# Fixed sort keys for the first part, latest-start keys behind it

## The chip, the cores and the metric

The kernel runs on one core of one Trainium2 chip. The metric is the device time of one execution in microseconds; a version is timed in several executions, and the median is given.

## What is computed

Three layers, each feeding the next, all in float32 on the inputs and outputs:

```python
# 1. retention: 4 batches, 8 heads, 576 positions, 64 dims
scores = scale * (q @ k.T)
ret = (scores * gamma ** rel where rel >= 0 else 0) @ v
x = ret, heads side by side              # 2304 x 512
# 2. first feed-forward layer, 512 -> 2048 -> 512
h = x @ w_in;  x = (h * cos(h)) @ w_out
# 3. second feed-forward layer, 512 -> 2048 -> 512
h = x @ w_in2; out = softplus(h) @ w_out2
```

## The kernel before

Matmuls work on pairs of a high and a low part of each operand (three products for one), so every activation and weight is split before use: ScalarE makes the high part, VectorE or GpSimd subtracts it to make the low one.

**The stages.** Retention is cut into 32 pieces (`piece`): scores (L625), running states (L630, L634), masks on VectorE (L652, L666), states on VectorE (L684), values (L702), then the split of the result into x (ScalarE L737, VectorE L349). The first 16 pieces run alone; the other 16 are spread over the first three of five token groups of layer 1's first part. That part, `moe_a`, multiplies each group by 4 of the 16 blocks of layer 1's weights: L789 into hidden units, then the chain ScalarE L824, VectorE L828, ScalarE L831, VectorE L834, ScalarE L859, VectorE L349 (`gl`), and L880 out of it. Its weights are made in SBUF by `weight` (ScalarE L423 and L429, VectorE L435, ScalarE L488 `wh`, VectorE or GpSimd L349 `wl`). The other blocks are converted ahead (`convert_ahead`: L423, L438, L442) and stored to DRAM. From then on the work is done in quads (L987, seven products in place of eight) with L1399 (layer 1) or L1150 (layer 2) multiplying out of them. The fifth group of the first part runs between the first quads.

**The order.** Nothing is ordered by hand. Every operation is entered into a `Plan` with an engine, a duration, a sort key and its tiles. `schedule` simulates the engines: at each step it takes the operation that can start earliest on its engine, and among those that could start at the same time the one with the smallest key. A piece of retention is one operation of TensorE there, so its readers count as ready when the whole piece is done. `latest` then walks backward from the planned TensorE times, works out how late each operation may begin, and writes that over the sort key of every ScalarE, VectorE and GpSimd operation; this is done twice before the last run of `schedule`. In that last run a second rule, with the constant `LOOK`, lets an operation go ahead of the chosen one if it would otherwise be late and the chosen one has room. The resulting order is emitted as the instruction streams; on the chip each engine works through its stream in that order and waits on semaphores. The chip does not know the planned times.

The fixed keys that matter here come from these lines, where `M[m]` is the nominal start of token group m (M[0] = M0 = 28.07) and a group's four slots are spaced by `slot_a(m)`, 7.02 for the first group:

```python
piece([i], [i], range(done, i), M[m] - 6.0 + y * FA * slot_a(m) / count)
        masks(i, K + 0.8)      # states: K + 0.4, after (x): K + 1.8
weight(1, f, W0[0] + W0[1] * f, W0[2])          # L435 at k + 0.6, wl at k + 2.8
        k = M[0] + CA[0] + 4 * i * CA[2]        # convert_ahead; L438 at k + 0.6
            op("dve", t_dve(n), K1 + 0.6, a2, ...)   # L828; K1 = slot start + 2.77
```

Of the kernel before, what the change touches and what calls it, by code (L numbers as in the profile page):

```python
# [66 lines left out]
    return layer == 2 or f < FA  # L67


FLEX = 1.332  # L70
FLEX_AD = 3.889
FLEX_2 = 50.0
ROOM = 258.786
SPARE = 1.248
# [6 lines left out]
GB = 2  # L81
PT = 3
R0 = 26.837
WB = (16.258, 19.07)
W3 = (33.511, 10.601, 13.324, 18.951, 18.328)
XW = 15.747
XC = 10.657
LAG_C = 1.399
LAG_S = 0.9
TT = 3  # L90
CA = (26.164, 78.45, 5.342, 6.693)
TURN = 0.6
XS = 51.414
FILL = (2, 5)
EARLY = 14.073
EARLY_2 = 4.87
PASSES = 2
LOOK = 0.5
LO_A = "pool or dve"
END = 3.1  # L100
LC = 8.411
LT = ("o", "s")
OFF = (-1.482, 8.354, 20.766, 32.756)
LL = 12.0
LB = 1.9
WARM = 350
DX = 24.051
LEAD = 7.302
W0 = (46.735, 4.619, -0.157)
M0 = 28.072  # L110
AK = (4.689, 2.82)
PAIR_A = 1.48
ALONE = 4
LENT = (0, 2)
# [3 lines left out]
KK = 1.331  # L118
KQ = -0.176
TIE = -8.153  # L120
LAG = -2.74
LEAD_G = 8.451
CX = 0.855
GT = (4, 7)
LS = 9
LEAD_S = 11.446
W4 = (-20.151, -4.061, 13.456, -5.221, 0.968)
W5 = (15.439, 11.845, 7.768, 11.854, 3.532)
PAD = 192
QS = 3  # L130

# [1 line left out]
class Plan:  # L133
# [65 lines left out]
    def latest(self, order, after):  # L199

        late, total = [0.0] * len(self.ops), max(self.end)
        for i in reversed(order):
            e, nbytes = self.eng[i], self.ops[i][6]
            if e == "pe":
                late[i] = self.start[i]
                continue
            lf = min((late[j] - (0.14 if self.eng[j] == e else self.LAT[e]) for j in after[i]), default=total)
            late[i] = lf - (1.7 + nbytes / 365e3 + LATE if nbytes else self.end[i] - self.start[i])
        for i, o in enumerate(self.ops):
            if self.eng[i] in ("act", "dve", "pool"):  # L210
                o[2] = late[i]
        return late

    def schedule(self, behind, loose, after, next_, late):
        n = len(self.ops)
        left = [0] * n
        for i, o in enumerate(self.ops):
            left[i] = len(o[4]) + len(behind[i])
        ready = [0.0] * n
        free, port, link = dict.fromkeys(("pe", "act", "dve", "pool", "sp", "host"), 0.0), 0.0, 0.0  # L220
        can = [i for i in range(n) if not left[i]]
        start, end, self.eng = [0.0] * n, [0.0] * n, [None] * n
        window, busy, warm = 0, 0.0, False
        for _ in range(n):
            best = None
            for i in can:
                eng, dur, key, _, _, uses_port, _ = self.ops[i]
                if eng == POOL_DVE:
                    f = max(ready[i], port)
                    t, d, e = min(  # L230
                        ((max(f, free[e]), d, e) for e, d in (("pool", t_pool(dur)), ("dve", t_dve(dur)))),
                        key=lambda o: o[0] + (FLEX if ready[i] < ROOM else FLEX_2 if ready[i] < ROOM_3 else FLEX_3) * o[1])
                elif eng == ACT_DVE:
                    t, d, e = min(
                        ((max(ready[i], free[e], port if e == "dve" and uses_port else 0.0), d, e) for e, d in zip(("act", "dve"), dur)),
                        key=lambda o: o[0] + FLEX_AD * o[1] + (SPARE if o[2] == "dve" else 0.0))
                else:
                    t, d, e = max(free[eng], ready[i], port if uses_port else 0.0, key - LEAD if eng == "sp" else 0.0), dur, eng
                k = (t, key, i, d, e)
                if best is None or k < best:  # L240
                    best = k
            assert best is not None, "the plan has a cycle"
            t, _, i, dur, eng = best
            if late and LOOK and eng in ("act", "dve"):
                more = None
                for j in can:
                    e, d, key = self.ops[j][:3]
                    if j != i and e == eng and ready[j] < t + dur:
                        f = max(free[eng], ready[j], port if self.ops[j][5] else 0.0)
                        if f < t + dur and late[j] < t + dur + LOOK and f + d + LOOK < late[i] and (more is None or (late[j], f, j) < more[0]):  # L250
                            more = (late[j], f, j), d
                if more:
                    (_, t, i), dur = more
            can.remove(i)
            what, _, _, _, _, uses_port, nbytes = self.ops[i]
            start[i], self.eng[i] = t, eng
            at, left_ = t, dur if eng == "pe" else 0.0
            while left_ > 1e-9:
                edge = (window + 1) * CLOCK_WINDOW
                if at >= edge:  # L260
                    warm = busy > (0.42 if warm else 0.75) * CLOCK_WINDOW
                    window, busy = window + 1, 0.0
                    continue
                run = min(edge - at, left_ * (1 if warm else 2))
                at, busy, left_ = at + run, busy + run, left_ - run / (1 if warm else 2)
            if eng == "pe":
                dur = at - t
            free[eng] = end[i] = t + dur
            if uses_port and eng != "act" or what == POOL_DVE:
                port = t + dur  # L270
            if nbytes:
                link = max(link, t + 1.7) + nbytes / 365e3
                end[i] = link + (0.95 if t < 60.0 else LATE)
            for j in next_[i]:
                ready[j] = max(ready[j], t)
                left[j] -= 1
                if not left[j]:
                    can.append(j)
            for j in after[i]:
                same = self.ops[j][0] == eng and not nbytes  # L280
                ready[j] = max(ready[j], end[i] + ((0.0 if (j, i) in loose else self.OWN.get(eng, 0.0)) if same else self.LAT[eng]))
                left[j] -= 1
                if not left[j]:
                    can.append(j)
        self.start, self.end = start, end
        return sorted(range(n), key=lambda i: (start[i], i))
# [11 lines left out]
def retention_moe_moe(ctx, tc, qkv, w1, w2, mask, mtail, dq, dk, out):  # L298
# [205 lines left out]
    def weight_out(q, key):  # L504
# [10 lines left out]
        for j in range(2):  # L515
            k = key + j * W3[4]
            ok, ov = oks[j], ovs[j]
# [442 lines left out]
    def quad(ph, y, s):  # L960
# [43 lines left out]
        product(1, 1, K, True, True)  # L1004
        op(ACT_DVE, both, K + DT - EARLY, keep(1, 0, "v"), r=[rk[1], ("qopen",)], w=[(cv, 0)], new=[("cv", 1, cv)])
        product(2, 2, K + DT, True, True)
        product(3, 5, K + 2 * DT, True, True)
        op("dve", t_dve(HN), K + 3 * DT - EARLY_2, lambda: nc.vector.tensor_tensor(R(2), R(2), c["v"][:, 0], ALU.add), r=[(cv, 0)], w=[rk[2]])
        op(ACT_DVE, both, K + 3 * DT - EARLY, keep(3, 0, "5"), r=[rk[3], ("qopen",)], w=[(cv, 0)])
        product(1, 6, K + 3 * DT)  # L1010
        op(ACT_DVE, both, K + 4 * DT - EARLY, keep(1, 1, "v"), r=[rk[1]], w=[(cv, 1)])
        product(3, 3, K + 4 * DT)
# [5 lines left out]

        op("dve", t_dve(HN), K + 6 * DT - EARLY, fourth, r=[rk[1], (cv, 0)], w=[rk[4]], new=free(4))
        op("dve", t_dve(HN), K + 5 * DT - EARLY_2, lambda: nc.vector.tensor_tensor(R(3), R(3), c["v"][:, 1], ALU.add), r=[(cv, 1)], w=[rk[3]])  # L1020
        product(1, 4, K + 6 * DT)
# [281 lines left out]
    def weight_in_s(ph, y, s):  # L1303
# [6 lines left out]
        wk = wof(ph, y, q)  # L1310
        W = (W3, W4, W5)[ph]
        slot_ = c % 2
        zd = NP2 * (layer - 1) + q
        made = (wk, "made")
        key = KI(ph, y, s) - (W[0] if y == 0 and s < 2 else W[1] if y == 0 or ph else XW)

# [304 lines left out]
    for i in range(P0):  # L1621
        k = M[0] + CA[0] + 4 * i * CA[2]
        job(k, convert_ahead, 1, FQ[0] + i, k, CA[2])
    for q in range(NP2):
        k = CM[0] + CA[1] + 4 * q * CA[3]
        job(k, convert_ahead, 2, q, k, CA[3])
    for ph in range(3):
        W = (W3, W4, W5)[ph]
        for y in range(nb):
            k = KI(ph, y, 0) - XC  # L1630
            job(k, x_load, ph, y, k)
            for s in range(NQ[ph]):
                job(KI(ph, y, s), quad, ph, y, s)
                job(KI(ph, y, s) - max(0.1, W[0] if y == 0 and s < 2 else W[1] if y == 0 or ph else XW), weight_in_s, ph, y, s)
                if not ph:
# [5 lines left out]
        for q in range(NQ[ph]):  # L1641
            if ph:
                job(key_s(ph, 0, 0, q) - max(W[4 if q > 1 else 2], 0.1), weight_out_s, ph, q)
            else:
                k = unit_key(0, 0, q) - W3[2]
                job(max(k, (MR if q < 2 else MB) + 0.01), weight_out, FQ[0] + q, k)
# [83 lines left out]
```

## Time and profile before

| what | value |
|---|---|
| median of 3 runs | 834.55 us (831.53 to 835.55) |
| the profiled execution's own time | 835.85 us |
| its span, first to last instruction | 834.1 us |
| TensorE busy | 818.9 us, 98% |
| VectorE / ScalarE / GpSimd busy | 665.3 / 513.3 / 76.6 us |
| mean granted clock of TensorE | 0.996 |

The profiled execution's own time is 1.75 us longer than the span. TensorE's busy time counts overlapping matmuls once, and a matmul at half clock is busy for twice as long, so the busy share says little on its own; the idle time and the granted clock by stretch say where time is lost.

### The profile page before, as it was taken

What the parts mean: (1) busy time and instruction counts of PE and PEld (TensorE: products, weight loads), DVE (VectorE), ACT (ScalarE), POOL (GpSimd) and SP (SyncE); (2) the same over time, 40 slices, a digit from 0 to 9 for tenths busy, and PEclk for the clock granted to TensorE, in tenths of its full rate; (3) what the DMA queues carried; (4) which work ended last, traced back from release to release, by engine and by line L of the source; (5) the groups of instructions that cost most, each with busy time, mean ns of one, the idle gap of its engine ahead of it and who ended that gap; (6) DMA issues with size and microseconds to landing.
All of it is one profiled execution on the core that took longest, in us unless ns stands there. A gap on an engine that the chain in (4) does not pass through costs nothing.

```text
span 834.1 us, 15908 instructions
## 1 busy us (share of the span) xinstructions
PE 818.9 (98%) x5792; PEld 781.5 (94%) x5792; DVE 665.3 (80%) x1486; ACT 513.3 (62%) x1128; POOL 76.6 (9%) x99
## 2 busy tenths in 40 slices
PE   8999999899999999999999999999999999999998
PEld 5777788888999999999999999999999999999998
DVE  3788667988989756876577889879788999876896
ACT  1275554567877866767767776555565766554551
POOL 3631010200402010010101010000000000000000
PEclk9999999999999999999999999999999999999999
DMA  9797999898788989486958967715558585563313
GB/s 302 297 353 242 333 395 325 295 397 323 286 306 257 340 305 328 156 231 230 299 200 261 312 213 224 264 66 204 214 175 329 210 303 199 175 233 127 139 51 114
DMA packets 74797, 208.78 MB, mean 250 GB/s; under 512 B 6880, under 2 KB 31072, under 8 KB 70880
## 3 DMA queue, kind: packets, MB, share of 16 engines
q1 hardware_dynamic: 71264, 203.06, 67.1%
q0 software_dynamic: 3456, 4.72, 3.8%
q8 instruction: 45, 0.74, 0.4%
q14 instruction: 32, 0.26, 0.1%
HBM read 129.64 MB, written 78.12 MB: 249 GB/s over the span
## 4 chain that ended last, share of the span: by engine, by line
PE 70%; DVE 1%; ACT 0%; DMA 0%; issue 0%; DVEq 0%
PE acc L1150 22%; PE ha L987 19%; PE acc L1399 16%; PE s L987 9%; PE hb L987 5%; DMA wr<-in_w 0%; DVE tt L1552 0%; DVE pair L349 0%; DVE er L828 0%; ACT pair L1270 0%; DVE s L1020 0%; DVE o L1017 0%; DVE gs L834 0%; ACT gh L859 0%; ACT wr L429 0%
## 5 line engine op out<-in xcount | busy, mean ns | idle before, releaser
L987 PE MATMUL ha<-x,pair 128*128 128x384 f32 x1008 | 202.8, 335 | 0.5 <-DVE o L1017 0.5
L987 PEld LDWEIGHTS ha<-x,pair 128*128 128x128 f32 x1008 | 174.5, 188 | 2.3 <-DVE o L1017 0.8
L1399 PE MATMUL acc<-gh,pair 128*128 128x384 f32 x576 | 155.4, 334 | 0.0
L1150 PE MATMUL acc<-pair,gh 128*128 128x256 f32 x544 | 106.7, 283 | 0.0
L1399 PEld LDWEIGHTS acc<-gh,pair 128*128 128x128 f32 x576 | 104.8, 188 | 0.0
L987 PE MATMUL s<-x,pair 128*128 128x384 f32 x504 | 101.2, 335 | 0.5 <-DVE gl L349 0.4
L1399 PE MATMUL acc<-gl,pair 128*128 128x384 f32 x288 | 96.4, 335 | 0.4 <-DVE gl L349 0.4
L987 PEld LDWEIGHTS s<-x,pair 128*128 128x128 f32 x504 | 88.0, 188 | 1.3 <-DVE gl L349 0.7
L1150 PEld LDWEIGHTS acc<-pair,gh 128*128 128x128 f32 x544 | 84.6, 191 | 0.0
L1150 PE MATMUL acc<-pair,ah 128*128 128x256 f32 x408 | 81.7, 281 | 0.0
L1150 PE MATMUL acc<-pair,gl 128*128 128x256 f32 x272 | 76.8, 282 | 0.0
L831 ACT ACTIVATE er<-er,hp_t 128x384 f32<-128x384 f32 (+1 forms) x92 | 57.4, 628 | 15.1 <-DVE er L828 14.7
L1150 PEld LDWEIGHTS acc<-pair,ah 128*128 128x128 f32 x408 | 66.5, 190 | 0.2 <-DVE pt L1197 0.2
L1150 PE MATMUL acc<-pair,al 128*128 128x256 f32 x204 | 57.7, 283 | 0.0
L353 ACT ACTIVATE cv<-ha 128x384 f32<-128x384 f32 x84 | 41.0, 488 | 26.4 <-PE ha L987 26.1
L349 DVE TENSOR_TENSOR gl<-sf,gh 128x512 fp32r<-128x512 f32 x68 | 46.9, 689 | 10.6 <-ACT gh L1128 9.9
L1399 PEld LDWEIGHTS acc<-gl,pair 128*128 128x128 f32 x288 | 54.1, 188 | 0.8 <-DVE gl L349 0.7
L1128 ACT ACTIVATE gh<-sf 128x512 fp32r<-128x512 f32 x68 | 43.0, 632 | 18.3 <-DVE sf L1093 12.4
L1150 PEld LDWEIGHTS acc<-pair,gl 128*128 128x128 f32 x272 | 52.0, 191 | 0.0
L987 PE MATMUL hb<-x,pair 128*128 128x384 f32 x252 | 50.6, 335 | 0.0
L423 ACT ACTIVATE wy<-wr 128x512 f32<-128x512 f32 x64 | 42.5, 665 | 8.8 <-DVE wk L435 3.1
L987 PEld LDWEIGHTS hb<-x,pair 128*128 128x128 f32 x252 | 43.6, 188 | 0.0
(209 smaller groups left out, 1684.1 us busy)
## 6 DMA issues: line engine op xcount, KB each, us to landing
wr<-in_w SPq DMA_DIRECT2D x64, 512.0 KB, 6.5
pair<-wpd SPq DMA_DIRECT2D x16, 1792.0 KB, 7.0
wpd<-pair SPq DMA_DIRECT2D x14, 1792.0 KB, 8.0
wd<-wk SPq DMA_DIRECT2D x56, 256.0 KB, 5.1
pair<-wd SPq DMA_DIRECT2D x36, 256.0 KB, 5.6
sd<-x SPq DMA_DIRECT2D x12, 768.0 KB, 4.3
x<-sd SPq DMA_DIRECT2D x12, 768.0 KB, 7.2
raw<-in_qkv SPq DMA_DIRECT2D x12, 640.0 KB, 6.9
```

What stands on the lines that cost most here:

```text
L349: e.tensor_tensor(out_, a, hi.bitcast(F32), ALU.subtract)
L353: nc.scalar.activation(out_, in_, AF.Copy)
L423: nc.scalar.activation(y, T["wr", u][:, :, 1].bitcast(F32), AF.Prelu, scale=2.0 ** -112, alpha=2.0 ** 32)
L831: nc.scalar.activation(e["r"], e["r"], AF.Sin, bias=hp_t[:, 0:1], scale=TWO_PI)
L987: nc.tensor.matmul(R(r), w_(a), x_(b), start=(start and n == 0), stop=(n == 5), skip_group_check=True)
L1128: nc.scalar.activation(T[hk], T[fk], AF.Copy)
L1150: nc.tensor.matmul(acc[m][:, i * 256:i * 256 + 256], l[p], r[o], start=(s == 0 and i == 0 and n == 0), stop=(s == half_p - 1 and n == 2), ...
L1399: nc.tensor.matmul(acc[m][:, 0:HN], l[:, z_], e[r], start=(first and z == 0), stop=(last and z == 2))
```

## The change

A constant `LATE_FROM = 150.0` is added, a time in the plan's own microseconds. Operations of ScalarE, VectorE and GpSimd that the plan starts before it keep the fixed key that they were entered with; only those after it get the latest-start key. The second rule (`LOOK`) works only behind that time too. That point lies at the end of the spread pieces of layer 1's first part, about where the first quad begins. Beside it 14 constants or tuples that make up keys and thresholds get new values. No operation is added or removed, and no tile, buffer count or transfer size is changed.

```diff
-FLEX = 1.332
-FLEX_AD = 3.889
+FLEX = 1.319
+FLEX_AD = 3.856
-WB = (16.258, 19.07)
-W3 = (33.511, 10.601, 13.324, 18.951, 18.328)
-XW = 15.747
-XC = 10.657
+WB = (16.86, 21.855)
+W3 = (33.09, 10.062, 18.026, 16.22, 18.284)
+XW = 18.07
+XC = 10.621
-CA = (26.164, 78.45, 5.342, 6.693)
+CA = (23.719, 75.53, 5.342, 4.427)
-EARLY = 14.073
-EARLY_2 = 4.87
+EARLY = 13.944
+EARLY_2 = 8.541
-LOOK = 0.5
+LOOK = 0.32
+LATE_FROM = 150.0
-OFF = (-1.482, 8.354, 20.766, 32.756)
-LL = 12.0
+OFF = (-1.221, 10.539, 20.766, 32.756)
+LL = 10.179
-W0 = (46.735, 4.619, -0.157)
+W0 = (46.735, 4.227, -0.157)
-AK = (4.689, 2.82)
+AK = (4.689, 2.701)
-LAG = -2.74
-LEAD_G = 8.451
+LAG = -3.013
+LEAD_G = 7.778
-LEAD_S = 11.446
-W4 = (-20.151, -4.061, 13.456, -5.221, 0.968)
-W5 = (15.439, 11.845, 7.768, 11.854, 3.532)
+LEAD_S = 10.241
+W4 = (-19.467, -8.868, 14.452, -5.177, 15.14)
+W5 = (16.461, 18.885, 9.073, 12.575, 2.839)
...
         for i, o in enumerate(self.ops):
-            if self.eng[i] in ("act", "dve", "pool"):
+            if self.eng[i] in ("act", "dve", "pool") and self.start[i] > LATE_FROM:
                 o[2] = late[i]
...
-            if late and LOOK and eng in ("act", "dve"):
+            if late and LOOK and eng in ("act", "dve") and t > LATE_FROM:
                 more = None
```

## Rows read from the trace of the kernel before

**Rows 1.** Busy time by engine in stretches, with granted clock (PEclk) and DMA share:

```profile
core 0: us, PE busy (x) PEld busy (x) DVE busy (x) ACT busy (x) POOL busy (x), PEclk, DMA share, GB/s
...
40.00:80.00 40.00, 36.47 (x361) 28.55 (x359) 35.06 (x82) 27.42 (x61) 8.90 (x12) 0.97 0.78 278
80.00:120.00 40.00, 40.00 (x297) 32.19 (x294) 26.32 (x64) 20.20 (x43) 3.55 (x6) 0.99 0.99 367
...
160.00:260.00 100.00, 96.12 (x513) 89.50 (x512) 90.31 (x158) 75.35 (x148) 16.23 (x13) 1.00 0.90 338
260.00:830.00 570.00, 570.00 (x3755) 569.27 (x3755) 458.31 (x1025) 361.14 (x801) 21.32 (x24) 1.00 0.64 218
```

**Rows 2.** Waits of TensorE: line waited for, us in total, times, longest:

```profile
PE s L625 <- DVE st L684: 3.5, 2, 2.0
PE o L789 <- DVE gl L349: 2.2, 1, 2.2
...
PE ha L987 <- DVE o L1017: 0.5, 1, 0.5
PE s L987 <- DVE gl L349: 0.4, 1, 0.4
PE acc L1399 <- DVE gl L349: 0.4, 1, 0.4
PE acc L880 <- ACT pt L353: 0.4, 1, 0.4
```

**Rows 3.** Busy time by engine behind the second stall, columns as in the first group:

```profile
76.00:81.00 5.00, 4.29 (x46) 3.46 (x47) 4.19 (x13) 1.84 (x3) 0.24 (x1) 0.66 0.98 298
```

**Rows 4.** Timeline of VectorE from 72.5 us: start, us, instruction, idle before it:

```profile
72.53 1.39 DVE L442 SCALAR_TENSOR_TENSOR wk<-wr,wk 128x512 int32<-128x512 int32 x1
73.85 0.68 DVE L828 CUSTOM_DVE_ANT_0 er<-ek,hb 128x512 f32<-128x512 int32 x1
74.45 0.41 DVE L652 TENSOR_TENSOR p<-s,m_t 128x256 f32<-128x256 f32 x1
74.78 0.27 DVE L684 SCALAR_TENSOR_TENSOR st<-st,dk_t,s 128x64 f32<-128x64 f32 x1
75.58 0.42 DVE L652 TENSOR_TENSOR p<-o,m_t 128x256 f32<-128x256 f32 x1 [0.54 <-ACT x L737]
...
76.39 0.27 DVE L684 SCALAR_TENSOR_TENSOR st<-st,dk_t,s 128x64 f32<-128x64 f32 x1
```

**Rows 5.** Timeline of ScalarE in the same stretch:

```profile
74.56 0.72 ACT L831 ACTIVATE er<-er,hp_t 128x512 f32<-128x512 f32 x1 [1.36 <-DVE er L828]
75.19 0.36 ACT L737 ACTIVATE x<-o 128x256 fp32r<-128x256 f32 x1
```

**Rows 6.** Timeline of TensorE around the second stall:

```profile
76.71 0.37 PE L625 MATMUL s<-raw 64*128 64x128 f32 x1 [2.04 <-DVE st L684]
```

**Rows 7.** Timeline of VectorE and TensorE around the first stall:

```profile
46.22 0.69 DVE L349 TENSOR_TENSOR wl<-wk,wh 128x512 fp32r<-128x512 f32 x1 [0.42 <-ACT wh L488]
46.83 0.42 DVE L652 TENSOR_TENSOR p<-s,m_t 128x256 f32<-128x256 f32 x1
...
47.87 0.37 PE L625 MATMUL s<-raw 64*128 64x128 f32 x1 [1.49 <-DVE st L684]
```

**Rows 8.** Timeline before a product of the first part that needs fresh weights:

```profile
59.85 2.08 DVE L349 TENSOR_TENSOR wl<-wk,wh 128x512 fp32r<-128x512 f32 x2
...
62.59 0.39 PE L789 MATMUL ha<-x,wl 128*128 128x512 f32 x1
```

**Rows 9.** L442 and L1552 on VectorE: durations min/median/max in ns, first and last start:

```profile
L442 DVE SCALAR_TENSOR_TENSOR wk<-wr,wk x17: 681/691/1391, 69.5 to 150.2; 128x512 int32<-128x512 int32 x17
...
L1552 DVE TENSOR_TENSOR tt<-tt x6: 952/954/2360, 162.4 to 259.8; 128x768 f32<-128x768 f32 x6
```

**Rows 10.** GpSimd beside the long L442 and beside the long L1552:

```profile
72.50 0.88 POOL L602 TENSOR_TENSOR qs<-raw,dq_t 128x320 f32<-128x320 f32 x1 [5.30 <-PE o L702]
...
162.15 1.84 POOL L1552 TENSOR_TENSOR tt<-x 128x768 f32<-128x768 f32 x1 [2.30 <-DVE gl L349]
```

## The prediction

> **What bounds the kernel now.** I read three views in turn: busy time by stretch, the waits of TensorE, and the timelines around the longest of these waits.
>
> The stretches come first because TensorE looks 98% busy as a whole, and the question is where the rest is. From 260 to 830 us it is busy for 570.00 of 570 us at a granted clock of 1.00 [rows 1]: that part is a rigid block, in which an order of the other engines can only lose. Nothing can be gained behind 260 us but the last 4 us. Ahead of it, 40 to 80 us has TensorE idle for 3.53 us while VectorE is busy for 35.06 of 40, and 160 to 260 us has it idle for 3.88 us while VectorE is busy for 90.31 of 100. From 80 to 120 us VectorE has room (26.32 of 40) and TensorE never idles. So VectorE's order matters in two stretches.
>
> The waits name the instructions: two stalls of 3.5 us together on the states of retention (L684), one of 2.2 us on `gl` of the first part's chain, and four of 0.5, 0.4, 0.4 and 0.4 us [rows 2]. That is 3.5 + 2.2 + 1.7 = 7.4 us. The clock adds a little: behind the second stall the stretch from 76 to 81 us has a mean granted clock of 0.66 [rows 3], that is, 3.4 us at 1.2 GHz among 2.4, which costs half of that, 1.7 us. In all some 9 us of 835.85 can be gained, 1.1%, and no order gives more.
>
> **The change part by part.** Work is neither added nor removed, so each step is a stall that goes, stays or appears. The sum is made against the profiled execution's 835.85 us (span 834.1 and 1.75 around it); the median, 834.55, is 1.30 lower, and the result is shifted by that.
>
> *The second stall (2.04 us, at 74.67 to 76.71).* Its place in the timeline: VectorE does L442, a conversion for much later, then L828 of the chain, and then the first mask; ScalarE meanwhile holds L831, which waits for L828 for 1.36 us, ahead of the x split of retention (L737), and the second mask follows that split at 75.58 [rows 4, 5]. TensorE's next piece starts only when the last state is made at 76.39 to 76.66 [rows 4, 6]. Now the fixed keys. This piece is the first of the second group: 28.07 + 4 x 7.02 - 6 + 0.8 = 50.95 for its masks and 50.55 for its states. The chain's L828, of the first group's fourth slot, has 28.07 + 3 x 7.02 + 2.77 + 0.6 = 52.50. The conversions have 28.07 + 23.72 + 0.8 = 52.59 for the first L442 and 5.34 more for each next one; the L442 at 72.53 is not the first, which starts at 69.5 [rows 9], so 57.93 or later. Retention therefore comes first wherever several are ready together, and the piece is done at 72.50, when GpSimd's L602, which waits for it, starts [rows 10]. The mask at 74.45 and the state then start near 72.5, and the x split (50.15 + 1.9 = 52.05) need not sit behind L831 (53.10). From the start of the second mask to the end of the last state it takes 76.66 - 75.58 = 1.08 us; begun at about 73.2 it ends before 74.67, when TensorE runs dry. I take the whole stall as gone, 2.04, and the 1.7 us of low clock with it, since in these rows the clock falls right behind the idle time. Together 3.7 us; the bounds are 0 (the stall is only handed to another piece) and 3.7.
>
> *The first stall (1.49 us, before 47.87).* The low half of a weight (`wl`) at 46.22 stands ahead of the mask at 46.83 [rows 7]. Here the keys agree too (22.07 + 0.8 for the mask, 46.74 + 2.8 for `wl`), but the key decides only among operations that could start at the same time, and the plan holds a piece's readers back until the whole piece is done, which is at 47.87 - 1.49 = 46.38 in the trace. `wl` was ready before that. At best the mask moves from 46.83 to 46.38: 0.45 us, which I take; the bounds are 0 and 1.49.
>
> *What is pushed back.* VectorE is 88% busy from 40 to 80 us [rows 1], so what goes first displaces something. Conversions for later lose nothing: from 80 us on there is room. The weights of the first part are another matter. Two `wl` end at 59.85 + 2.08 = 61.93 and the product that reads one starts at 62.59 [rows 8], 0.66 us later. One piece's work on VectorE takes 0.41 + 0.27 us for the first mask and state and 1.08 us from the second mask to the last state, 1.76 us [rows 4]; put ahead of a `wl`, it uses that slack up and makes a stall of 1.1 us. I take one such stall, +1.1. Bounds: 0, as the new W0 lowers the weights' keys by 0.39 for each step from block to block, and 3.3 for blocks 1 to 3.
>
> *Behind 150 of the plan's time.* I take the boundary to be near the first quad, some 161 us in the trace. The third stall (2.15) lies behind it, so the old rule still orders it, with other keys around it. I take 0 here, with bounds of -3.9 (third stall and the four small ones gone) and +3.9 (as much again). From 260 us on I take 0 as well: what hides the changed order there is TensorE's own backlog, as no wait shows in 570 us [rows 1].
>
> The sum: -3.7 - 0.45 + 1.1 = -3.05 us, so 832.8 as the profile would have it and 831.5 us as a median.
>
> *A rule to weigh.* One L442 took 1391 ns where the median is 691, and one L1552 took 2360 where the median is 954 [rows 9]; each ran beside a GpSimd instruction that had started just before, at 72.50 and at 162.15 [rows 10]. That is 0.70 us in front of the second stall and 1.41 in front of the third. The Trainium skill, SBUF — State Buffer, section "Who interferes with whom", says that a VectorE instruction with both inputs in SBUF and a GpSimd instruction that reads SBUF share one port, which the first holds to its end while the other is blocked. These two rows agree with that within 0.2 us (72.50 + 0.88 + 0.69 = 74.07, where the end is 73.92), though the second may as well wait for GpSimd's result. By that rule alone sort keys would cure only what is not lock time, and L602, which GpSimd starts when a piece ends, would go on blocking whatever VectorE reads from SBUF then.
>
> **The rivals.**
>
> *The stalls only move.* The key is the second criterion, behind the earliest start, and the plan's times are not the chip's. If GpSimd's L602 (start 72.50, at a piece's end) meets some other VectorE instruction with two SBUF inputs in every order, 0.70 us stays in the 74 us stall and 1.41 in the third, and a different piece pays the rest. The time is then the old one within 1 us: 833.5 to 835.5. For it: the first stall, which the keys hardly touch. Against it: masks read one input from PSUM, and in the fixed order they would stand there in place of L442. This is also the case in which the change doesn't do what it says.
>
> *All of it goes.* The old rule works from a plan whose start is out of step with the chip; with a steadier start the third stall and the small ones go too: -3.7 - 0.45 - 3.9 = -8.05, half of which to all of which gives 826.5 to 830.5. For it: a clean block from 260 us on shows that the old rule is good once there is backlog. Against it: VectorE is 90% busy from 160 to 260 us [rows 1].
>
> *Slower: weights late.* With retention and the chain ahead of them in key (50.95 for the masks above, against 46.74 + 2 x 4.23 + 2.8 = 58.0 for `wl` of block 2), blocks 1 to 3 of the first part each come late by a whole piece's 1.76 us, after 0.66 us of slack: 3 x 1.1 = 3.3 us, and if the clock falls again 1.7 or 3.4 us more. Where the old stalls stay as well this is +3.3 to +6.7: 838 to 841; where they go, 834 to 837. It decides from the point where a `wl` ends later than 62.6 us less the earlier gain. For it: the 0.66 us. Against it: the smaller W0 step, and VectorE's short idle times there.
>
> **How the numbers follow.** The chances: partly cured, as summed, 0.44 (830.4 to 833.5, the upper end with two late weights); all gone 0.18 (826.5 to 830.5); moved 0.20 (833.5 to 835.5); weights late 0.18 (834 to 841). The likeliest gives 831.5 us. The range of 8 in 10 leaves out the upper part of the last case and the far end of the second: 827 to 838. About 0.5%, 4.2 us here, is what a measurement of this kernel can tell from no change (the three runs before lie 4.0 us apart), so faster means below 830.4 and slower above 838.7. Faster gets the second case and a little over a quarter of the first, since runs spread by as much as its gain: 0.31. Slower gets over half of the fourth, 0.11; the rest, 0.58, is within it.
>
> **What would show it.** Right: no TensorE idle time over 0.5 us between 65 and 80 us, granted clock 1.00 there, masks (L652) ahead of L442 and L828, L737 ahead of L831, and 570 us of block as before. Wrong: a wait of L789 on `wl` between 54 and 68 us (weights late); the 2 us wait on L684 at another piece (moved); a wait of L987, L1399 or L1150 behind 260 us, which would mean that the new keys took slack that no row shows; or a third stall gone, which would put the gain where I put none.

## The result and the profile after

The changed kernel took 839.36 us as a median of 5 executions (836.6 to 840.64), the kernel before 833.59 us beside it (5 executions, 831.5 to 835.55). The ratio is 1.0067, with an interval from 1.0044 to 1.0090. The change made the kernel slower by 0.7%; the forecast was 831.5 us, and 839.36 lies above its range.

The change gives 19 constants or tuples new values, not 14 as said above. The profiled execution after took 839.16 us, its span is 837.4 us. All line numbers after are one higher than before. Busy time by stretch with the columns of [rows 1], first before, in the stretches that the readings below need:

```profile
40.00:60.00 20.00, 18.51 (x233) 14.34 (x230) 17.00 (x49) 14.33 (x37) 6.08 (x9) 1.00 0.89 333
60.00:80.00 20.00, 17.96 (x129) 14.21 (x130) 18.06 (x34) 13.09 (x25) 2.83 (x4) 0.93 0.67 223
...
160.00:200.00 40.00, 37.48 (x190) 33.65 (x189) 35.65 (x61) 27.24 (x52) 4.42 (x3) 1.00 0.96 375
200.00:260.00 60.00, 58.65 (x325) 55.84 (x324) 54.67 (x97) 48.11 (x97) 11.80 (x10) 1.00 0.86 313
```

Then after; the row from 76 us answers to [rows 3]:

```profile
40.00:60.00 20.00, 17.98 (x173) 13.56 (x169) 14.27 (x40) 12.50 (x33) 5.53 (x7) 0.83 0.90 323
60.00:80.00 20.00, 20.00 (x163) 15.38 (x163) 18.21 (x39) 13.37 (x25) 3.79 (x5) 1.00 0.69 211
...
76.00:81.00 5.00, 5.00 (x56) 3.82 (x55) 4.84 (x14) 1.44 (x3) 0.91 (x2) 1.00 0.97 288
...
160.00:200.00 40.00, 38.80 (x191) 33.99 (x191) 36.42 (x62) 26.89 (x51) 3.99 (x3) 1.00 0.98 377
200.00:260.00 60.00, 55.83 (x304) 52.43 (x303) 53.91 (x91) 46.52 (x94) 16.14 (x13) 1.00 0.86 312
260.00:830.00 570.00, 569.54 (x3740) 568.03 (x3740) 458.58 (x1022) 362.62 (x803) 21.35 (x24) 1.00 0.63 217
```

Read TensorE's busy time (first figure behind the comma) and the granted clock together. From 60 to 80 us TensorE never idles now (before: 17.96 of 20 at a clock of 0.93), and from 160 to 200 us it is idle for 1.20 us (before 2.52). Against that stand two losses. From 40 to 60 us the idle time went from 1.49 to 2.02 us and the clock from 1.00 to 0.83, which is 0.17 x 20 = 3.4 us. From 200 to 260 us, where the trace of before has 1.35 us of idle time, there are 4.17, and GpSimd works 16.14 us there in place of 11.80. From 260 to 830 us there are 0.46 us of idle time where before there were none.

Of these two losses the second is the one that shows in the difference between the two spans, 3.3 us. The clock took about as much from the execution before: 1.7 us behind the second stall, and it stood at 0.96 over the first 40 us (after: 1.00), which is another 1.6. Up to 200 us the changed kernel is not behind: its TensorE has 1722 matmuls by then, before 1715, counted without regard to their size. From 200 to 260 us it has 304, at the same clock of 1.00, and before 325. At 60 / 325 = 0.185 us each, the 21 missing ones are an estimated 3.9 us.

The waits of TensorE after, which answer to [rows 2]:

```profile
PE s L626 <- ACT x L738: 2.0, 1, 2.0
...
PE hb L988 <- DVE pair L350: 1.4, 1, 1.4
PE ha L988 <- ACT cv L354: 1.3, 2, 0.9
...
PE acc L881 <- DVE gl L350: 0.9, 1, 0.9
PE s L988 <- DVE gs L835: 0.7, 1, 0.7
PE s L988 <- ACT cv L354: 0.7, 2, 0.5
```

The two waits on L684, 3.5 us together, and the one of 2.2 us on `gl` are gone. One wait of retention is left, 2.0 us, and what ends it is ScalarE's split of the result (L738), no longer VectorE's state; all lines with L988 are waits of quads, and none of [rows 2] for a quad was longer than 0.5 us.

The first stall, after, in the timelines of VectorE and TensorE, which answer to [rows 7]:

```profile
45.41 0.95 DVE L350 TENSOR_TENSOR wl<-wk,wh 128x512 fp32r<-128x512 f32 x1
46.28 0.27 DVE L685 SCALAR_TENSOR_TENSOR st<-st,dk_t,s 128x64 f32<-128x64 f32 x1
46.47 0.41 DVE L653 TENSOR_TENSOR p<-s,m_t 128x256 f32<-128x256 f32 x1
...
46.98 0.58 PE L626 MATMUL s<-raw 64*128 64x128 f32 x2 [1.98 <-ACT x L738]
...
48.90 1.07 PE L703 MATMUL o<-p,raw 128*64 128x128 f32 x8
```

The weight `wl` still goes ahead of the masks, as it did before. The eight products of L703 take 1.07 us; at full clock they take 0.61 (a row of e7 below), so half the clock made them 1.75 times as long here. So the piece behind this stall ran at 1.2 GHz.

### The profile page after: what moved, and what is told of

It reads as the page before. It is cut to its first block, busy times and chain, and to the rows that moved or that the text cites. A ratio compares the mean times of both kernels' runs of the same rounds, so it can differ in the third digit from the quotient of the medians.

```text
span 837.4 us, 15889 instructions
## 1 busy us (share of the span) xinstructions
PE 822.4 (98%) x5792; PEld 781.8 (93%) x5792; DVE 667.8 (80%) x1482; ACT 514.5 (61%) x1128; POOL 81.5 (10%) x103
## 4 chain that ended last, share of the span: by engine, by line
PE 87%; DVE 7%; ACT 2%; DMA 2%; issue 1%; SPq 0%; POOL 0%; DVEq 0%; ACTq 0%; POOLq 0%
PE acc L1151 22%; PE ha L988 19%; PE acc L1400 16%; PE s L988 10%; PE acc L881 5%; PE hb L988 5%; PE ha L790 2%; PE hb L790 2%; PE o L703 2%; PE s L626 1%; DVE pair L350 1%; DVE gl L350 1%; PE s L631 1%; DVE tt L1294 1%; DMA dq_t<-in_dq 1%
## 5 line engine op out<-in xcount | busy, mean ns | idle before, releaser
L988 PE MATMUL ha<-x,pair 128*128 128x384 f32 x1008 | 203.4, 336 | 1.8 <-ACT cv L354 1.3
L988 PEld LDWEIGHTS ha<-x,pair 128*128 128x128 f32 x1008 | 174.3, 188 | 4.9 <-ACT cv L354 2.4
L988 PE MATMUL s<-x,pair 128*128 128x384 f32 x504 | 101.4, 335 | 1.4 <-DVE gs L835 0.7
L988 PEld LDWEIGHTS s<-x,pair 128*128 128x128 f32 x504 | 88.1, 188 | 2.6 <-ACT cv L354 1.4
L832 ACT ACTIVATE er<-er,hp_t 128x384 f32<-128x384 f32 (+1 forms) x92 | 57.7, 627 | 13.8 <-DVE er L829 12.8
L988 PE MATMUL hb<-x,pair 128*128 128x384 f32 x252 | 50.9, 335 | 1.4 <-DVE pair L350 1.4
L1009 DVE TENSOR_TENSOR hb<-hb,cv 128x384 f32<-128x384 f32 x42 | 23.7, 564 | 31.2 <-PE hb L988 28.9
```

What stands on the lines that cost most here:

```text
L832: nc.scalar.activation(e["r"], e["r"], AF.Sin, bias=hp_t[:, 0:1], scale=TWO_PI)
L988: nc.tensor.matmul(R(r), w_(a), x_(b), start=(start and n == 0), stop=(n == 5), skip_group_check=True)
```

## The experiments

Two theories stood at the start: the loss is in the rule (keys and second rule switched off before 150 us of the plan), or it is in the new constants. Each kernel was timed beside the kernel before. In the table, "idle" is 60 less TensorE's busy time from 200 to 260 us, "GpSimd" its busy time there (both of the profiled execution), and "clock" the mean granted clock over all executions of that kernel. "At full clock" is an estimate that takes the clock out: the median of each execution's time multiplied by its own granted clock. In the 129 executions of the kernel before beside the experiments, the time rises by 0.8 us for each 0.001 that the clock is lower, so nearly all that the clock withholds is paid in time. The clock of one execution is known to 0.0005, which is 0.4 us.

| kernel | median us | ratio to before, interval | idle | GpSimd | clock | at full clock |
|---|---|---|---|---|---|---|
| before | 833.6 to 835.4 | 1 | 1.35 | 11.80 | 0.997 | 832.4 to 832.9 |
| changed | 839.36 | 1.0067 (1.0044 to 1.0090) | 4.17 | 16.14 | 0.997 | 836.9 |
| e1 | 839.88 | 1.0063 (1.0043 to 1.0082) | 2.49 | 11.56 | 0.996 | 836.5 |
| e2 | 835.03 | 1.0008 (0.9992 to 1.0023) | 2.15 | 9.37 | 0.999 | 833.9 |
| e3 | 837.03 | 1.0032 (1.0014 to 1.0050) | 3.45 | 8.40 | 0.996 | 834.0 |
| e4 | 840.43 | 1.0070 (1.0047 to 1.0093) | 1.60 | 14.39 | 0.995 | 835.6 |
| e5 | 839.27 | 1.0046 (1.0024 to 1.0068) | 2.90 | 12.31 | 0.996 | 835.1 |
| e6 | 836.41 | 1.0021 (1.0003 to 1.0039) | 2.03 | 15.06 | 0.998 | 834.9 |
| e7 | 834.07 | 1.0000 (0.9980 to 1.0020) | 2.13 | 9.57 | 0.998 | 832.8 |
| e8 | 835.24 | 1.0005 (0.9986 to 1.0023) | 1.20 | 12.80 | 0.997 | 832.9 |
| e9 | 834.91 | 1.0009 (0.9989 to 1.0030) | 1.58 | 11.39 | 0.998 | 833.5 |
| e10 | 838.49 | 1.0054 (1.0039 to 1.0068) | 4.17 | 15.79 | 0.998 | 836.9 |
| e11 | 834.00 | 0.9993 (0.9978 to 1.0007) | 1.69 | 11.40 | 0.998 | 832.2 |
| e12 | 833.08 | 0.9988 (0.9972 to 1.0003) | 2.49 | 12.51 | 0.999 | 832.4 |
| e13 | 842.29 | 1.0096 (1.0079 to 1.0114) | 1.19 | 7.21 | 0.994 | 837.7 |
| e14 | 840.01 | 1.0070 (1.0055 to 1.0084) | 4.58 | 16.21 | 0.997 | 837.5 |
| e15 | 835.51 | 1.0013 (0.9998 to 1.0029) | 2.22 | 9.59 | 0.997 | 833.7 |
| e16 | 836.49 | 1.0037 (1.0021 to 1.0052) | 4.39 | 15.28 | 0.999 | 835.9 |
| e17 | 834.23 | 0.9983 (0.9960 to 1.0006) | 0.86 | 5.76 | 0.997 | 831.3 |
| e18 | 832.56 | 0.9957 (0.9937 to 0.9978) | 1.15 | 7.00 | 0.998 | 831.2 |

**Rule or constants: e1 to e4.** e1 has the rule with the constants of before; e2 the new constants without the rule; e3 gives back the old values to the constants of the quads, e4 to those of the first part.

```diff
 # e2
-LATE_FROM = 150.0
+LATE_FROM = -1.0
 # e1: all 19; e3: WB W3 XW XC EARLY EARLY_2 LOOK LAG LEAD_G LEAD_S W4 W5
 # e4: FLEX FLEX_AD CA OFF LL W0 AK
-FLEX = 1.319
+FLEX = 1.332
...
```

> The kernel before with the 150 us boundary alone; all constants as before. Keys theory (the loss of the change comes from the new constants that shape the work around the quads): TensorE's idle time from 200 to 260 us as before, about 1.5 us, and a median of 830 to 834 us. Rule theory (fixed keys in the first part cost the time, whatever the constants): a stall of 2 us or more near 46 us with the clock low behind it, and 837 to 841 us.

> The changed kernel with the boundary at -1, so that latest-start keys hold from the beginning as before; all constants as changed. Keys theory: idle time from 200 to 260 us stays at 4 us or more, and the median is 836 to 841 us. Rule theory: the first 60 us go as before and the median is 831 to 835 us.

> The changed kernel with the constants of the quads' work (WB, W3, XW, XC, EARLY, EARLY_2, LOOK, LAG, LEAD_G, LEAD_S, W4, W5) as before; those of the first part and the boundary as changed. Keys theory: the idle time from 200 to 260 us is back to about 1.5 us and the median at 832 to 836 us, the difference to the changed kernel being the 4 to 5 us lost there. Rule theory: no change, 837 to 841 us.

> The changed kernel with the constants of the first part (FLEX, FLEX_AD, CA, OFF, LL, W0, AK) as before; those of the quads' work and the boundary as changed. Keys theory: 837 to 841 us with 4 us or more of idle time from 200 to 260 us, and the stall near 46 us may be shorter than 2 us. Rule theory: 837 to 841 us as well, with the stall near 46 us as in the changed kernel.

The rule costs the time: e1, the rule alone, is as slow as the changed kernel, and e2, the constants alone, is as fast as the kernel before. No group of old constants brings it all back: e3 about half, e4 nothing by its median. e1 and e4 have little idle time from 200 to 260 us, so what they lose lies elsewhere in part (in e4, 3.4 us of idle time behind 260 us); the place found below is that of the changed kernel's own order. In e1, e2 and the changed kernel alike TensorE is busy for 20.00 of 20 us from 60 to 80 us, so the second stall goes with the rule and also without it: either part of the change is enough.

**Where: e5, e6, e9, e10, and which half of the rule: e7, e8.** The rule does two things before 150 us: fixed keys in place of latest-start keys, and no second rule (`LOOK`).

```diff
 # e5: LATE_FROM = 60.0.  e6: both halves only between 60 and 150.
 # the second rule is switched on again ...
-            if late and LOOK and eng in ("act", "dve") and t > LATE_FROM:
+            if late and LOOK and eng in ("act", "dve"):                               # e7: everywhere
+            if late and LOOK and eng in ("act", "dve") and not 60.0 < t <= LATE_FROM:  # e9
+            if late and LOOK and eng in ("act", "dve") and t > 60.0:                   # e10
 # e8: the latest-start keys are used everywhere, the second rule behind 150 only
-            if self.eng[i] in ("act", "dve", "pool") and self.start[i] > LATE_FROM:
+            if self.eng[i] in ("act", "dve", "pool"):
```

> The changed kernel with the boundary at 60 in place of 150, so that only the retention that runs alone and the first spread pieces have fixed keys. If the fixed keys cost their time in the first 60 us (the stall near 46 us and the low clock behind it): 837 to 841 us. If they cost it between 60 and 150, by what they leave behind at the boundary: 833 to 836 us, with 2 us less idle time from 200 to 260 us than in the changed kernel.

> The changed kernel with fixed keys only between 60 and 150; ahead of 60 latest-start keys, as behind 150. If the first 60 us cost the time: 833 to 836 us. If the stretch from 60 to 150 does: 837 to 841 us, with 4 us or more idle from 200 to 260 us and a stall near 46 us of 1.5 us as before. If neither half alone does, both runs stand between 835 and 838 us.

> The changed kernel with the second rule (LOOK) at work from the beginning; keys fixed up to 150. If it is the missing second rule that costs the time: 833 to 836 us. If it is the fixed keys: 837 to 841 us.

> The changed kernel with latest-start keys from the beginning and the second rule only behind 150: the other half of the rule. If the fixed keys cost the time: 833 to 836 us, as with the boundary at -1 (835.0). If the missing second rule does: 837 to 841 us.

> The changed kernel with the second rule (LOOK) at work ahead of 60 and behind 150, not between; keys fixed up to 150. If the second rule earns its time in the first 60 us: 833 to 836 us, with 2 us or more less lost between 40 and 60 us than in the changed kernel. If it earns it between 60 and 150: 837 to 841 us.

> The mirror image: the second rule from 60 on, not ahead of it; keys fixed up to 150. If the second rule earns its time in the first 60 us: 836 to 841 us, with the stall near 46 us and the low clock behind it. If it earns it between 60 and 150: 833 to 836 us.

Neither half costs anything alone: with the second rule back (e7) or the latest-start keys back (e8) the time is that of before. Only both together cost, and what matters is whether the second rule works in the first 60 us of the plan: e9 has it there and takes 834.91, e10 lacks it there and takes 838.49. From 200 to 260 us e10 has the idle time of the changed kernel, though the second rule works in it from 60 us on. e5 and e6, with both halves, settle nothing: their ratios differ the same way, but their intervals overlap, at full clock they are within 0.2 us, and e6 at 836.41 fits only its third expectation, which e5 at 839.27 misses.

What the second rule does there can be seen in e7 beside the first stall (timelines of GpSimd, VectorE and TensorE of e7):

```profile
46.42 1.26 POOL L350 TENSOR_TENSOR wl<-wk,wh 128x512 fp32r<-128x512 f32 x1 [0.45 <-ACT wh L489]
46.46 0.42 DVE L653 TENSOR_TENSOR p<-s,m_t 128x256 f32<-128x256 f32 x1
47.17 0.28 DVE L685 SCALAR_TENSOR_TENSOR st<-st,dk_t,s 128x64 f32<-128x64 f32 x1 [0.29 <-ACT st L681]
...
47.51 0.48 PE L626 MATMUL s<-raw 64*128 64x128 f32 x2 [1.48 <-DVE st L685]
...
48.76 0.61 PE L703 MATMUL o<-p,raw 128*64 128x128 f32 x8
...
49.09 0.68 DVE L350 TENSOR_TENSOR wl<-wk,wh 128x512 fp32r<-128x512 f32 x1
```

The first `wl` is now made on GpSimd, so VectorE begins with the mask; the `wl` at 49.09 is that of the next block. The stall is 1.48 us in place of 1.98, and the clock does not fall. The stall had not become shorter than before [rows 7]: there `wl` went first on VectorE and it was 1.49.

**Two better sets: e11 and e12.** e11 is e7 with the old constants of the quads; e12 has latest-start keys and the second rule everywhere and new values only for the first part's constants.

> Fixed keys up to 150 as in the change, the second rule from the beginning, the constants of the quads' work as before and those of the first part as changed: the parts that have come out best so far. If the three gains add up: 830 to 833 us, faster than the kernel before by up to 0.5%. If the second rule alone was what was missing: 833 to 835 us.

> Latest-start keys and the second rule from the beginning, as in the kernel before, with the constants of the first part alone as changed. If the old quad constants are the better ones whatever the rule (the changed kernel with them took 837.0 us against 839.4): 831 to 834 us. If they are better only where the second rule is missing: 834 to 836 us.

Both are as fast as before, and no gain is shown: the interval of each holds 1. The kernel without the second stall gains nothing that can be measured.

**The order ahead or the order behind: e13 to e16.** Most of TensorE's idle time behind 40 us in the changed kernel's trace lies behind 200 us, yet what decides is in the first 60. These kernels take the changed kernel's order for what is planned to begin ahead of a cut and e7's order behind it, or the reverse.

```diff
+        (head, start, eng_h), (rest, _, eng_r) = plans     # the changed kernel's and e7's
+        first = {i for i in head if start[i] < CUT}        # CUT: 150 (e13, e14), 60 (e15, e16)
+        self.eng = [eng_h[i] if i in first else eng_r[i] for i in range(n)]
+        return [i for i in head if i in first] + [i for i in rest if i not in first]
```

> All constants as in the changed kernel. What is planned to begin before 150 us is issued in the changed kernel's order, the rest in the order of the kernel that looks ahead everywhere (834.1 us). If the loss belongs to the order written for the time behind 150 us, this one is near 834, from 833 to 836 us, and TensorE is idle for some 2 us between 200 and 260 us. If the first part leaves the kernel in a state that costs it later, whatever the order behind, it is from 837 to 840 us with some 4 us idle there.

> The reverse: the order of the kernel that looks ahead everywhere up to 150 us, the changed kernel's order from there on. If the loss belongs to the order behind 150 us: from 837 to 840 us, and some 4 us idle between 200 and 260 us. If it is left behind by the first part: from 833 to 836 us and some 2 us idle.

> The changed kernel's order for what is planned to begin before 60 us, then that of the kernel that looks ahead everywhere. If the order of the first 60 us itself costs the time: from 837 to 840 us. If it costs only by the other orders that are planned behind it: from 833 to 836 us.

> The reverse: looking ahead in the first 60 us, then the changed kernel's own order. If the order of the first 60 us itself costs the time: from 833 to 836 us. If it costs only by the orders planned behind it: from 837 to 840 us.

With the changed order behind, the idle time is there whatever goes ahead: 4.39 us in e16 and 4.58 in e14. With e7's order behind it isn't: 2.22 in e15 and 1.19 in e13. The waits of TensorE of e16 from 200 to 260 us (lines ten higher than after) are those of the changed kernel:

```profile
PE ha L998 <- ACT cv L364: 1.6, 2, 1.2
PE hb L998 <- DVE pair L360: 1.4, 1, 1.4
PE s L998 <- DVE gs L845: 0.7, 1, 0.7
```

The four kernels e7, e15, e16 and the changed one are a table of two by two, by ratio 1.0000, 1.0013, 1.0037 and 1.0067. The order behind 60 us costs 0.37 to 0.54%, 3.1 to 4.5 us; the order of the first 60 us itself costs 0.13 to 0.30%, 1.1 to 2.5 us. Each ratio is known to some 0.2%, so the first is clearly there, and the second is so only as far as it makes the difference between e16 and the changed kernel. At full clock the four are 832.8, 833.7, 835.9 and 836.9: 3.1 to 3.2 us for the order behind and some 1 us for the order ahead, so that part of the second cost is clock. e16 at 836.49 falls between its two expectations, as it would where both orders cost. e13 fits neither expectation: it has little idle time behind 200 us and still takes 842.29. Two orders joined at 150 us leave 2.48 us idle from 80 to 160 us and 2.09 from 160 to 200, where the changed kernel has 0.00 and 1.20, so the joint itself costs, and e13 decides nothing; nor does the time of e14, which leaves 1.80 us idle from 80 to 160 us.

**GpSimd in the order behind: e17, e18.** Three of the waits behind 200 us have the same history. In the timelines of the changed kernel from 212 us:

```profile
212.22 1.69 POOL L350 TENSOR_TENSOR pair<-wr,pair 128x512 fp32r<-128x512 f32 x1 [4.90 <-PE ha L988]
212.67 1.78 DVE L350 TENSOR_TENSOR pair<-wr,pair 128x512 fp32r<-128x512 f32 x1
...
215.91 0.54 DVE L835 TENSOR_TENSOR gs<-s,er 128x384 f32<-128x384 f32 x1
216.51 1.34 PE L988 MATMUL s<-x,pair 128*128 128x384 f32 x6 [0.73 <-DVE gs L835]
...
227.14 1.38 POOL L350 TENSOR_TENSOR pair<-wr,pair 128x512 fp32r<-128x512 f32 x1 [13.23 <-DMA x<-xdl]
227.30 1.51 DVE L1294 TENSOR_TENSOR tt<-tt,pair 128x256 f32<-128x256 f32 x1
...
230.00 0.68 DVE L350 TENSOR_TENSOR pair<-pair 128x512 fp32r<-128x512 f32 x1
...
230.73 0.97 PE L988 MATMUL hb<-x,pair 128*128 128x384 f32 x4 [1.36 <-DVE pair L350]
```

A VectorE row of 1.78 us where its shape takes 0.68, and one of 1.51 where its shape takes 0.42, each beside a GpSimd row that began just before. VectorE works without a gap from the long row to the one that TensorE waits for, so nothing on the way absorbs its 1.10 and 1.09 us. The third place has two such rows (1.10 and 1.22 us where 0.55 and 0.68 are usual), again with no gap on VectorE up to the row whose result ScalarE turns into what TensorE waits for:

```profile
232.92 1.97 POOL L1294 TENSOR_TENSOR tt<-pair 128x256 f32<-128x256 f32 x2
233.20 1.10 DVE L350 TENSOR_TENSOR gl<-g,gh 128x384 fp32r<-128x384 f32 x1
...
234.22 1.22 DVE L350 TENSOR_TENSOR pair<-wr,pair 128x512 fp32r<-128x512 f32 x1
...
236.49 1.32 PE L988 MATMUL s<-x,pair 128*128 128x384 f32 x6 [0.46 <-ACT cv L354]
```

e17 takes GpSimd's sums out of this stretch of the changed kernel's plan; e18 does so in e7, as a control.

```diff
+QUIET = (190.0, 235.0)
...
-                        ((max(f, free[e]), d, e) for e, d in (("pool", t_pool(dur)), ("dve", t_dve(dur)))),
+                        ((max(f, free[e]), d, e) for e, d in (("pool", t_pool(dur)), ("dve", t_dve(dur)))
+                         if e == "dve" or not (late and QUIET[0] < f < QUIET[1])),
```

> The changed kernel, whose sums of weights that may run on GpSimd or VectorE are all given to VectorE from 190 to 235 us of the plan; the order up to there is the changed kernel's. In the changed kernel the trace shows GpSimd busy there beside three VectorE rows of 1.78, 1.51 and 1.10 us, where others of the same shapes take 0.68, 0.42 and 0.55 us. If these long rows make the idle time behind 200 us: 2 to 3 us less idle time of TensorE from 200 to 260 us and 836 to 837.5 us. If it is only the order of VectorE's own work: no less idle time, 838.5 to 840 us.

> The same silence of GpSimd in the kernel that looks ahead everywhere (834.1 us), as a control. There GpSimd has half as much to do in this stretch; if GpSimd's share is what differs, this one changes by less than 1 us: 833.5 to 835 us. If VectorE can't bear the added work: 836 us or more.

e17 takes 834.23 us, lower than expected, and the stretch from 200 to 260 us in it reads:

```profile
200.00:260.00 60.00, 59.14 (x337) 58.17 (x336) 55.98 (x107) 49.38 (x100) 5.76 (x4) 1.00 0.84 308
```

VectorE has 107 instructions there in place of 91 and is busy for 2.07 us more only, TensorE's idle time falls from 4.17 to 0.86 us, and it has 337 matmuls there in place of 304. VectorE's groups by shape from 200 to 240 us show why; first the changed kernel, then e17 (lines two higher), with count, busy time and mean ns of one:

```profile
L350 DVE TENSOR_TENSOR pair<-wr,pair 128x512 fp32r<-128x512 f32 x8 | 7.1, 888 | 0.0
L350 DVE TENSOR_TENSOR gl<-g,gh 128x384 fp32r<-128x384 f32 x6 | 3.9, 645 | 0.2 <-ACT gh L860 0.2
L1294 DVE TENSOR_TENSOR tt<-tt,pair 128x256 f32<-128x256 f32 x2 | 1.9, 962 | 0.0
```

```profile
L352 DVE TENSOR_TENSOR pair<-wr,pair 128x512 fp32r<-128x512 f32 x10 | 6.7, 683 | 0.0
L352 DVE TENSOR_TENSOR gl<-g,gh 128x384 fp32r<-128x384 f32 x8 | 4.4, 552 | 0.2 <-ACT gh L862 0.2
L1296 DVE TENSOR_TENSOR tt<-tt,pair 128x256 f32<-128x256 f32 x3 | 1.3, 418 | 0.0
```

VectorE did ten sums of 128x512 in less time than eight before. e17 still has the first stall (1.97 us, as in the changed kernel) and is not slower than the kernel before. The control misses its expectation: e18 is faster than e7, 832.56 us, with a ratio of 0.9957 whose interval ends at 0.9978. So GpSimd's sums cost time in that stretch of e7 too, though less (its idle time falls from 2.13 to 1.15). At full clock the silence of GpSimd is worth 1.6 us in e7 (832.8 to 831.2) and 5.6 in the changed kernel (836.9 to 831.3). Both kernels also plan VectorE's work anew behind 190 us; that the long rows are the cause, and not the new plan, rests on the three places above, which hold 2.55 us (0.73, 1.36 and 0.46) of the 3.3 that went. The wait on `cv`, 0.94 us at 204.90 in the changed kernel, stays in e17 with 0.86. e18 has the lowest median of this study. Against the kernel before, part of its gain is clock: at a mean clock of 1.000 its five executions have a median of 831.64 us, and the 22 of the kernel before 832.72.

GpSimd's busy time alone does not tell the loss: e6 has 15.06 us of it from 200 to 260 us and only 2.03 of idle time. It counts where one of its rows meets VectorE ahead of a row that TensorE waits for.

## Why the prediction was wrong

**The step that failed: "Behind 150 of the plan's time".** It took 0, because "the old rule still orders it". The rule there is the same, but its result isn't: it starts from another state of the plan and gives more of the weight sums to GpSimd. The order behind 60 us costs 3.1 to 4.5 us (two by two, above), and without GpSimd's sums from 190 to 235 us of the plan the changed kernel no longer pays it (e17). Two of the prediction's own signs of being wrong show it: the third stall went, where it had put no gain (1.20 us of idle time from 160 to 200 us, before 2.52), and L988 waits for 0.46 us behind 260 us. The bounds of +-3.9 us were about right; the 0 between them had no reason from a row. Why a first part without the second rule leads the planner to give GpSimd more was not tested.

**What was not costed: the second rule before 150.** The prediction weighed fixed keys against latest-start keys only. e7 and e8 show that keys alone cost nothing; the second rule's absence on top of them does. Its cost in the first 60 us itself is 1.1 to 2.5 us, at full clock some 1 us.

**The second stall** went, as predicted: no idle time from 60 to 80 us, clock 1.00 from 76 to 81 us where [rows 3] have 0.66. But it did not go by the step that was predicted. These rows after answer to [rows 4], [rows 5] and [rows 10]:

```profile
73.27 0.68 DVE L443 SCALAR_TENSOR_TENSOR wk<-wr,wk 128x512 int32<-128x512 int32 x1
73.97 0.69 DVE L829 CUSTOM_DVE_ANT_0 er<-ek,hb 128x512 f32<-128x512 int32 x1
74.69 0.72 ACT L832 ACTIVATE er<-er,hp_t 128x512 f32<-128x512 f32 x1 [0.76 <-DVE er L829]
...
75.08 0.42 DVE L653 TENSOR_TENSOR p<-s,m_t 128x256 f32<-128x256 f32 x1
75.14 0.88 POOL L603 TENSOR_TENSOR qs<-raw,dq_t 128x320 f32<-128x320 f32 x1 [4.48 <-PE o L703]
75.32 0.37 ACT L738 ACTIVATE x<-o 128x256 fp32r<-128x256 f32 x1
```

The order is the old one: the conversion, then the chain's L829, then the mask, and on ScalarE L832 ahead of the split. Two signs of being right, masks ahead of both and L738 ahead of L832, are missing. What differs is the piece: it ends 2.64 us later (GpSimd's L603 starts at 75.14, before at 72.50). By then the conversion and the chain's row are done, and the conversion takes 0.68 us in place of 1.39, with L603 no longer beside it. The mask starts with the piece's end; before it came 1.95 us behind it. So the idle time in this term was right in size by luck.

The credit for it was also too large. The stall goes with either part of the change (e1, e2), so fixed keys aren't needed for it. And e7 and e11, which have this gain and little idle time behind (2.13 and 1.69 us, before 1.35), are at 1.0000 and 0.9993. Part of the 3.7 us was the 1.7 us of clock, which the kernel before does not pay each time: of its 129 executions beside the experiments 22 had a mean granted clock of 1.000, and their median is 832.72 us; in e7 five had it, with a median of 832.95.

**The first stall** was taken as 0.45 us shorter. It is 0.49 us longer (1.98). The mask did not move ahead of `wl`, and VectorE is not what TensorE waits for in the end: the state is done at 46.28 + 0.27 = 46.55, and TensorE starts at 46.98, released by ScalarE's split. With the second rule `wl` goes to GpSimd and the stall is 1.48 (e7). Behind the longer stall the clock fell in the profiled execution after, 3.4 us that no step had. That is not the loss as a median, though: the mean clock over all executions is 0.997 before and after, and the profiled execution before lost as much to the clock in other places. At equal clock of 1.000 the one execution after took 836.6 us, and e16, with the changed order behind, took 835.8 to 836.7 in seven.

**What is pushed back** was wrong: no product L790 waits between 50 and 70 us, so there is no stall for late weights, and +1.1 was not there. The rival *slower: weights late* gave 838 to 841 us, and the time fell into it, but by none of its mechanism.

**A rule to weigh.** The rows of the changed kernel bear it out in another place than where the prediction looked. 212.22 + 1.69 + 0.68 = 214.59, where the long row ends at 212.67 + 1.78 = 214.45; and 227.14 + 1.38 + 0.42 = 228.94, where it ends at 228.81. Both rows end as if VectorE had started when GpSimd ended. The Trainium skill, SBUF — State Buffer, section "Who interferes with whom", says that a VectorE instruction with two inputs in SBUF and a GpSimd instruction that reads SBUF share one port, which one holds to its end. These rows agree within 0.2 us. The prediction held this against a cure of the second stall. It should have asked for the whole stretch in which the new order can put a GpSimd row ahead of the chain.

## What to carry to other kernels

A rule of a planner that is switched off for the first part changes the order of all that comes after, although the rule there is the same: put a price on the far part as well, by its own slack, and not 0. Where VectorE is some 90% busy and its results go straight to TensorE, a sum handed to GpSimd can cost VectorE more than it saves (1.10 us of delay for a sum that VectorE does in 0.68): look for VectorE rows of two to three times their usual length, and try the stretch without GpSimd. A stall that is cured in one profiled execution is worth what it costs as a median, so set off the share of it that is clock. And a stall that went is no proof of the reason given for it: look at the order of the rows as well.

## What the hardware showed

From 200 to 240 us VectorE needed 6.7 us for ten sums of 128x512 with GpSimd silent (e17) and 7.1 us for eight where GpSimd ran beside some of them (the changed kernel). And the clock did not follow the length of a stall alone: behind 1.97 and 1.98 us of idle time at 47 us it fell in the profiled executions of e17 and of the changed kernel (mean clock of 40 to 60 us 0.91 and 0.83), while in e15 the same stall of 1.98 us and in e8 one of 2.35 us left it at 1.00, and in e16 one of 1.48 us stands in a stretch of 0.91.
